# Keys and values of a linear attention laid out as head by 64 partitions with nine tokens each

## The chip, the cores and the metric

The kernel runs on one core of a Trainium2 chip. The metric is the device time of one execution in microseconds; the median of several runs counts. A core has five engines with queues of their own: PE (matrix products; PEld is its weight load), DVE (vector), ACT (scalar functions), POOL and SP. SP issues the transfers that this kernel makes between the chip's main memory and the core's, which has 128 partitions. PE writes its products to PSUM, in banks of 512 fp32 numbers a partition.

## What is computed

The attention is linear: `k` is normalized by a softmax along the 576 tokens, `q` along the 64 features, and a 64x64 matrix `kv` stands between them. The result feeds two dense stages of experts.

```python
# q, k, v: (4, 8, 576, 64): batch, heads, tokens, features
q_s = exp(q - max(q, axis=-1)); q_s = q_s / (sum(q_s, axis=-1) + 1e-09)
k_s = exp(k - max(k, axis=2));  k_s = k_s / (sum(k_s, axis=2) + 1e-09)
kv = einsum('bhsd,bhse->bhde', k_s, v)         # sum over the tokens s: (b, h, 64, 64)
attn = einsum('bhsd,bhde->bhse', q_s, kv)
x = attn.transpose(0, 2, 1, 3).reshape(2304, 512)
x = ((x @ w1) * (x @ w2)) @ w3 @ w_out         # 512 -> 1024 -> 1024 -> 512
p = probs / (sum(probs, axis=-1) + 1e-09)
out = sum over the 4 experts e of p[:, e] * (relu(x @ w1[e]) @ w2[e])
```

## The kernel before

The heads are worked on in pairs `hp`, four pairs to a batch `b`, in the order `PAIRS = [0, 2, 1, 3]`. Each pair passes through these steps.

- `load_k` and `load_v` bring keys and values. Partition p holds tokens 4p to 4p+3 of both heads, 512 numbers; the 64 tokens left over stand in a fifth place `[0:KX, :, KR]` of partitions 0 to 63, by a transfer of their own. Each value tile has a column of ones behind the 64 features (written by POOL), so that the product gives the softmax's sum along with `kv`. In batch 0 the values go to a staging tile `vs` first, and ACT copies them.
- `k_max` takes the maximum over the tokens: three maxima on DVE (L239, L243, L244) leave 128 numbers a partition, PE transposes them (L246), DVE reduces them to one column (L250), PE spreads this column over all partitions by a product with the identity (L252), and ACT copies it to `mx` (L258).
- `k_exp` subtracts `mx` (DVE, L270) and takes the exponential (ACT, L273), twice each, for the four places and the fifth.
- `k_v` (batches 0 and 1) sums `kv` of both heads in five products of 128x128 weights by 130 columns, the two diagonal blocks of which are used. `k_v2` (batches 2 and 3, `JOINED = 2`) takes two pairs together, in twenty products with 64 columns of weights (L321), one head to each half of the array's columns. Their order is fixed by `after_inst`.

DVE then adds 1e-9 to the sums and inverts them, ACT scales the blocks into `bd`, and `x_stage` multiplies `bd` by the transposed queries (L405). Where a step stands in the program is set by slots: `K_SLOT`, `Q_SLOT` and `X_SLOT` give each batch's slots, `put` enters a step there, and between the slots' steps lie the dense products. Batch 0 runs alone at the start. Batch 1 runs among the first products `ab` (x by w1 and w2), while DVE and ACT convert and split the weights `f` into `wg` (L144 to L155, L103, L104). Batches 2 and 3 run among the products `y`. `mm3` makes each of these products as three (L109 to L111), for a high and a low part of the operands. Within this a scheduler of the compiler chooses each engine's order by its own estimate of times; `hold` and `after_inst` add edges to it. SP's queue holds all loads in their order. `keep_busy` issues products on ones among the steps of batch 0.

## Time and profile before

| what | value |
|---|---|
| median of 3 runs | 1141.66 us (1141.65 to 1142.82) |
| profiled execution | 1142.81 us, its span 1141.0 us |
| granted clock of PE, mean | 0.995 |
| attention, batch 0 | to about 32 us |
| batch 1, among the products `ab` | about 32 to 98 us |
| batch 2, among `W` and `y` | about 147 to 250 us |
| batch 3, among `ab` and `y` | about 250 to 305 us |
| experts | from about 424 us |

The busy share of an engine says how near it is to setting the time of a stage; the chain of waits says which work ended last. A row of the timeline gives start and length of one run of like instructions. Products are pipelined, so lengths overlap, and what a product costs is read from the starts of the products around it. The start of a product that follows one of another kind is modelled early; the sum over a few products is sound. A product in fp32 shows as two.

### The profile page before, as it was taken

The page shows a single profiled execution, that of the slowest core. Times are in us where ns is not written, and L with a number is a line of the kernel's source. Part 1 is how long each engine was busy: PE and PEld are TensorE (multiplying, and loading weights), DVE is VectorE, ACT ScalarE, POOL GpSimd, SP SyncE. Part 2 cuts the span into 40 slices and gives each one's busy share as a digit, 9 for nine tenths or more (in the row PEclk, how much of TensorE's full clock was granted, in tenths as well). Part 3 has the DMA queues.
Part 4 walks back from the last instruction along what each step waited for, and adds up shares of the span by engine and source line. Part 5 has one row for each costly group of instructions (what it writes and reads, how often), then busy time and mean ns, then how long its engine had stood idle before and what let it go on. Part 6 is the DMA issues. An engine that isn't in the chain of part 4 may idle for free.

```text
span 1141.0 us, 18926 instructions
## 1 busy us (share of the span) xinstructions
PE 1120.9 (98%) x7159; PEld 1044.8 (92%) x7159; DVE 869.1 (76%) x1460; ACT 534.7 (47%) x974; POOL 11.4 (1%) x54
## 2 busy tenths in 40 slices
PE   7899999999999999999999999999999999999998
PEld 5677888878888889999999999999999999999998
DVE  7999696856565527999989997777779877777777
ACT  4775245745453326645555444444435434443441
POOL 0000000000010000000000000000000000000000
PEclk8999999999999999999999999999999999999999
DMA  9987962899989768777777888777777797777774
GB/s 266 269 334 289 294 174 83 222 339 396 338 283 396 301 240 311 285 281 272 290 262 289 290 305 289 248 256 251 253 253 249 251 307 249 254 251 250 253 246 128
DMA packets 124667, 308.04 MB, mean 270 GB/s; under 512 B 27936, under 2 KB 51488, under 8 KB 124576
## 3 DMA queue, kind: packets, MB, share of 16 engines
q1 hardware_dynamic: 123616, 306.04, 77.9%
q8 instruction: 57, 0.93, 0.3%
q10 hardware_dynamic: 960, 0.79, 0.3%
q14 instruction: 34, 0.28, 0.1%
HBM read 230.24 MB, written 76.55 MB: 269 GB/s over the span
## 4 chain that ended last, share of the span: by engine, by line
PE 91%; DVE 4%; DMA 3%; SPq 1%; issue 1%; ACT 0%; DVEq 0%; ACTq 0%
PE hp L976 30%; PE op L1053 29%; PE ab L111 5%; PE ab L110 5%; PE ab L109 5%; PE y L110 3%; PE y L111 3%; PE y L109 3%; PE W L109 1%; PE W L110 1%; PE W L111 1%; DMA eg<-e_b 1%; PE xp L405 1%; DMA vt<-in_v_dram 1%; PE kv L294 1%
## 5 line engine op out<-in xcount | busy, mean ns | idle before, releaser
L1053 PE MATMUL op<-eg,h 128*128 128x256 f32 x3024 | 379.8, 280 | 0.8 <-DMA eg<-e_b 0.8
L976 PE MATMUL hp<-t,eg 128*128 128x384 f32 x2016 | 376.9, 336 | 0.9 <-DVE acc L1034 0.9
L1053 PEld LDWEIGHTS op<-eg,h 128*128 128x128 f32 x3024 | 373.5, 188 | 1.2 <-PE hp L976 1.1
L976 PEld LDWEIGHTS hp<-t,eg 128*128 128x128 f32 x2016 | 344.6, 188 | 2.9 <-DVE acc L1034 1.8
L1034 DVE SCALAR_TENSOR_TENSOR acc<-op,prob,acc 128x256 f32<-128x256 f32 (+1 forms) x399 | 197.9, 525 | 42.0 <-PE op L1053 41.9
L103 ACT ACTIVATE h<-blk 128x768 fp32r<-128x768 f32 x168 | 138.0, 843 | 143.1 <-DVE blk L673 108.9
L104 DVE TENSOR_TENSOR h<-blk,h 128x768 fp32r<-128x768 f32 x168 | 157.2, 951 | 24.4 <-ACT h L103 24.3
L959 ACT ACTIVATE blk<-hp 128x384 f32<-128x384 f32 x192 | 90.4, 489 | 141.6 <-PE hp L976 138.1
L963 DVE TENSOR_TENSOR blk<-hp,blk 128x384 f32<-128x384 f32 x144 | 79.3, 556 | 67.0 <-PE hp L976 66.6
L109 PE MATMUL ab<-x,wg 128*128 128x512 f32 (+1 forms) x320 | 120.0, 378 | 1.5 <-ACT bd L308 1.1
L110 PE MATMUL ab<-x,wg 128*128 128x512 f32 (+1 forms) x320 | 118.6, 371 | 1.6 <-ACT x L426 1.4
L111 PE MATMUL ab<-x,wg 128*128 128x512 f32 (+1 forms) x320 | 117.9, 371 | 0.3 <-DVE wg L104 0.3
L965 ACT ACTIVATE blk<-blk 128x768 f32<-128x768 f32 x72 | 60.6, 845 | 73.0 <-DVE blk L963 71.3
L673 DVE TENSOR_TENSOR blk<-blk 128x768 f32<-128x768 f32 x96 | 91.4, 952 | 0.5
L110 PEld LDWEIGHTS ab<-x,wg 128*128 128x128 f32 x320 | 60.3, 189 | 13.1 <-ACT x L426 3.0
L109 PEld LDWEIGHTS ab<-x,wg 128*128 128x128 f32 x320 | 60.1, 189 | 12.7 <-ACT bd L308 1.3
L111 PEld LDWEIGHTS ab<-x,wg 128*128 128x128 f32 x320 | 60.3, 189 | 10.5 <-DVE wg L104 0.7
L567 DVE TENSOR_TENSOR ah<-ab,ah 128x512 f32<-128x512 f32 (+1 forms) x40 | 25.2, 631 | 39.3 <-PE ab L111 39.3
L104 DVE TENSOR_TENSOR eo<-e2r,eo 128x512 fp32r<-128x512 f32 x56 | 37.7, 683 | 20.0 <-ACT eo L103 19.8
L111 PE MATMUL y<-h,W 128*128 128x512 f32 x128 | 50.4, 397 | 0.0
L110 PE MATMUL y<-h,W 128*128 128x512 f32 x128 | 50.4, 394 | 0.0
L109 PE MATMUL y<-h,W 128*128 128x512 f32 x128 | 49.2, 401 | 0.0
(107 smaller groups left out, 1004.2 us busy)
## 6 DMA issues: line engine op xcount, KB each, us to landing
eg<-e_t SPq DMA_DIRECT2D x96, 512.0 KB, 4.5
eg<-e_b SPq DMA_DIRECT2D x72, 512.0 KB, 5.0
eg<-e_s SPq DMA_DIRECT2D x68, 512.0 KB, 4.4
eg<-e_a SPq DMA_DIRECT2D x51, 512.0 KB, 4.6
wg<-w SPq DMA_DIRECT2D x44, 512.0 KB, 8.3
f<-in_moe_w_dram SPq DMA_DIRECT2D x32, 512.0 KB, 6.7
e_t<-eo SPq DMA_DIRECT2D x32, 512.0 KB, 7.5
e_s<-eg SPq DMA_DIRECT2D x28, 512.0 KB, 4.5
```

The costliest lines, as they stand in the source:

```text
L103: i = nc.scalar.activation(out=hi, in_=src, func=ACTF.Copy)
L104: j = eng.tensor_tensor(out=lo, in0=src, in1=hi.bitcast(F32), op=ALU.subtract)
L109: nc.tensor.matmul(out=ps, lhsT=w_hi, rhs=r_hi, start=first, stop=False, **kw)
L110: nc.tensor.matmul(out=ps, lhsT=w_hi, rhs=r_lo, start=False, stop=False, **kw)
L111: return nc.tensor.matmul(out=ps, lhsT=w_lo, rhs=r_hi, start=False, stop=last, **kw)
L673: return lambda: nc.vector.tensor_tensor(out=dst, in0=x, in1=y, op=op)
L959: nc.scalar.activation(out=block(name)[:, u], in_=src, func=func)
L963: nc.vector.tensor_tensor(out=x[:, u], in0=src, in1=x[:, u], op=ALU.add)
L965: nc.scalar.activation(out=x, in_=x, func=ACTF.Relu)
L976: nc.tensor.matmul(out=q, lhsT=w[:, sw, kt, P * u:P * u + P], rhs=t[b][:, kt, st], start=new and kt == 0 and i == 0, stop=kt == 1 and i == ...
L1034: nc.vector.scalar_tensor_tensor(out=dst, in0=src, scalar=prob[:, T, e:e + 1], in1=dst, op0=ALU.mult, op1=ALU.add,)
L1053: nc.tensor.matmul(out=q[:, c:c + DH], lhsT=g[:, sh, u, P * i:P * i + P], rhs=w[:, sw, u], start=new and u == 0 and j == 0, stop=u == 1 an ...
```

## The change

Partition 64h + p now holds the nine tokens 9p to 9p+8 of head h of the pair, 576 numbers without a rest.

- Transfers: one for keys and one for values of a pair. A partition's keys are 2304 bytes in a row. The staging tile of batch 0 is one for each pair.
- Maximum: one reduction over the nine tokens, which reads `p r d` as `p d r`, so with steps of 64 numbers. The transposed result has 64 rows; its reduction gives a column for each head, and two products of 64x64 spread them, each on its half of the partitions.
- One subtraction and one exponential a pair.
- `kv`: 18 products of 64x64 weights by 65 columns a pair, with head h on half h of the array's rows and of its columns. One function serves one pair (batches 0 and 1) or two (2 and 3). The products stay chained, now within a pair.
- POOL no longer clears the rest's padding.

```diff
     def load_k(b, hp):
-        t = ap_.tile([P, 2, KR + 1, D], F32, tag="kr", name="kr", bufs=4)
-        src = k[b, 2 * hp:2 * hp + 2]
+        t = ap_.tile([P, QR, D], F32, tag="kr", name="kr", bufs=4)
         hold("pace" if b > 2 else ("in", b), nc.sync.dma_start(
-            out=t[:, :, 0:KR], in_=src[:, 0:KR * P].rearrange("h (p r) d -> p h r d", p=P)
-        ))
-        hold("pace" if b > 2 else ("in", b), nc.sync.dma_start(
-            out=t[0:KX, :, KR], in_=src[:, KR * P:S].rearrange("h p d -> p h d")
+            out=t, in_=k[b, 2 * hp:2 * hp + 2].rearrange("h (p r) d -> (h p) r d", p=QP)
         ))
         kraw[b, hp] = t
 
-    staged = {}
-
     def load_v(b, hp):
-        t = ap_.tile([P, 2, KR + 1, D + 1], F32, tag="vt", name="vt", bufs=4)
+        t = ap_.tile([P, QR, D + 1], F32, tag="vt", name="vt", bufs=4)
         nc.gpsimd.memset(t[..., D:D + 1], 1.0)
-        if b >= JOINED:
-            nc.gpsimd.memset(t[KX:P, :, KR, 0:D], 0.0)
-        src = v[b, 2 * hp:2 * hp + 2]
+        src = v[b, 2 * hp:2 * hp + 2].rearrange("h (p r) d -> (h p) r d", p=QP)
+        x = t[..., 0:D]
         if b in V_WHOLE:
-            i = PAIRS.index(hp)
-            if i % 2 == 0:
-                staged[b] = raw("vs")
-            x = staged[b][:, 512 * (i % 2):512 * (i % 2) + 512].rearrange(
-                "p (h r d) -> p h r d", h=2, d=D
-            )
-            hold(("in", b), nc.sync.dma_start(
-                out=x, in_=src[:, 0:KR * P].rearrange("h (p r) d -> p h r d", p=P)
-            ))
-            nc.scalar.activation(out=t[:, :, 0:KR, 0:D], in_=x, func=ACTF.Copy)
-        for h in range(0 if b in V_WHOLE else 2):
-            hold("pace" if b > 2 else ("in", b), nc.sync.dma_start(
-                out=t[:, h, 0:KR, 0:D], in_=src[h, 0:KR * P].rearrange("(p r) d -> p r d", p=P)
-            ))
-        hold("pace" if b > 2 else ("in", b), nc.sync.dma_start(
-            out=t[0:KX, :, KR, 0:D], in_=src[:, KR * P:S].rearrange("h p d -> p h d")
-        ))
+            x = raw("vs")[:, 0:QR * D].rearrange("p (r d) -> p r d", d=D)
+        hold("pace" if b > 2 else ("in", b), nc.sync.dma_start(out=x, in_=src))
+        if b in V_WHOLE:
+            nc.scalar.activation(out=t[..., 0:D], in_=x, func=ACTF.Copy)
         vt[b, hp] = t
...
     def k_max(b, hp):
-        kr = kraw[b, hp]
-        m4 = ap_.tile([P, 2, 2, D], F32, tag="m2", name="m2", bufs=1)
-        i = hold(("k", b, PAIRS.index(hp)), nc.vector.tensor_tensor(
-            out=m4, in0=kr[:, :, 0:2], in1=kr[:, :, 2:4], op=ALU.max
+        m2 = ap_.tile([P, D], F32, tag="mf", name="mf", bufs=2)
+        hold(("k", b, PAIRS.index(hp)), nc.vector.tensor_reduce(
+            out=m2, in_=kraw[b, hp].rearrange("p r d -> p d r"), axis=AX.X, op=ALU.max
         ))
-        m2 = ap_.tile([P, 2, D], F32, tag="mf", name="mf", bufs=2)
-        nc.vector.tensor_tensor(out=m2, in0=m4[:, :, 0], in1=m4[:, :, 1], op=ALU.max)
-        nc.vector.tensor_tensor(out=m2[0:KX], in0=m2[0:KX], in1=kr[0:KX, :, KR], op=ALU.max)
         ps = bank(ps_a, "mt")
-        i = nc.tensor.transpose(ps[:, 0:P], m2.rearrange("p h d -> p (h d)"), ident)
+        i = nc.tensor.transpose(ps[0:D, 0:P], m2, ident)
         if b == 0:
             keep_busy(FILL_T[PAIRS.index(hp)], i)
-        mt = ap_.tile([P, 1], F32, tag="mt", name="mt", bufs=2)
-        nc.vector.tensor_reduce(out=mt, in_=ps[:, 0:P], axis=AX.X, op=ALU.max)
-
-        i = nc.tensor.matmul(
-            out=ps[:, P:2 * P], lhsT=mt.to_broadcast([P, P]), rhs=ident, start=True, stop=True
-        )
+        mt = ap_.tile([D, 2, 1], F32, tag="mt", name="mt", bufs=2)
+        nc.vector.tensor_reduce(
+            out=mt, in_=ps[0:D, 0:P].rearrange("d (h p) -> d h p", h=2), axis=AX.X, op=ALU.max
+        )
+        for h in range(2):
+            i = nc.tensor.matmul(
+                out=ps[D * h:D * h + D, P:P + D], lhsT=mt[:, h].to_broadcast([D, D]),
+                rhs=ident[0:D, 0:D], start=True, stop=True,
+            )
         if b == 0:
             keep_busy(FILL_B[PAIRS.index(hp)], i)
-        mx = ap_.tile([P, 2, 1, D], F32, tag="mx", name="mx", bufs=2)
-        nc.scalar.activation(
-            out=mx.rearrange("p h r d -> p (h r d)"), in_=ps[:, P:2 * P], func=ACTF.Copy
-        )
+        mx = ap_.tile([P, 1, D], F32, tag="mx", name="mx", bufs=2)
+        nc.scalar.activation(out=mx[:, 0], in_=ps[:, P:P + D], func=ACTF.Copy)
         mxk[b, hp] = mx
 
     def k_exp(b, hp):
         kr, mx = kraw.pop((b, hp)), mxk.pop((b, hp))
-        t = ap_.tile([P, KR + 1, 2, D], F32, tag="ek", name="ek", bufs=2)
-        if b >= JOINED:
-            nc.gpsimd.memset(t[KX:P, KR], 0.0)
-        for p, r0, n in ((P, 0, KR), (KX, KR, 1)):
-            x = kr[0:p, :, r0:r0 + n]
-            hold(("e", b, PAIRS.index(hp)), nc.vector.tensor_tensor(
-                out=x, in0=x, in1=mx[0:p].to_broadcast([p, 2, n, D]), op=ALU.subtract
-            ))
-            nc.scalar.activation(
-                out=t[0:p, r0:r0 + n].rearrange("p r h d -> p h r d"), in_=x, func=ACTF.Exp
-            )
+        t = ap_.tile([P, QR, D], F32, tag="ek", name="ek", bufs=2)
+        hold(("e", b, PAIRS.index(hp)), nc.vector.tensor_tensor(
+            out=kr, in0=kr, in1=mx.to_broadcast([P, QR, D]), op=ALU.subtract
+        ))
+        nc.scalar.activation(out=t, in_=kr, func=ACTF.Exp)
         ekt[b, hp] = t
...
-    def k_v(b, hp):
-        ek, vv = ekt.pop((b, hp)), vt.pop((b, hp))
-        bd = empty_bd()
-        ps = bank(ps_w if b == 0 else ps_a, "kv")
-        for r in range(KR + 1):
-            p = P if r < KR else KX
-            i = nc.tensor.matmul(
-                out=ps[:, 0:2 * D + 2], lhsT=ek[0:p, r].rearrange("p h d -> p (h d)"),
-                rhs=vv[0:p, :, r, :], start=r == 0, stop=r == KR,
-            )
-        if b == 0:
-            keep_busy(FILL_V[PAIRS.index(hp)], i)
-        rs = ap_.tile([P, 1], F32, tag="rs", name="rs", bufs=2)
-        nc.vector.tensor_scalar(
-            out=rs, in0=ps[:, D:D + 1], scalar1=1e-9, scalar2=None, op0=ALU.add
-        )
-        nc.vector.reciprocal(out=rs, in_=rs)
-        for h in range(2):
-            p = slice(D * h, D * h + D)
-            o = (D + 1) * h
-            nc.scalar.activation(
-                out=bd[p, D * h:D * h + D], in_=ps[p, o:o + D], func=ACTF.Copy, scale=rs[p]
-            )
-        kvb[b, hp] = bd
-
-    def k_v2(b, j):
-        ps = bank(ps_a, "kv").rearrange("p (w c) -> p w c", c=P)
-        bds, last = [], None
-        for hh in range(2):
-            bds.append(empty_bd())
-            ek, vv = ekt.pop((b, 2 * hh + j)), vt.pop((b, 2 * hh + j))
-            for r in range(KR + 1):
+    def k_v(b, *pairs):
+        ps = bank(ps_w if b == 0 else ps_a, "kv").rearrange("p (w c) -> p w c", c=P)
+        n = len(pairs)
+        for w, hp in enumerate(pairs):
+            ek, vv, last = ekt.pop((b, hp)), vt.pop((b, hp)), None
+            for r in range(QR):
                 for h in range(2):
+                    p = slice(D * h, D * h + D)
                     i = nc.tensor.matmul(
-                        out=ps[D * h:D * h + D, hh, 0:D + 1], lhsT=ek[:, r, h], rhs=vv[:, h, r],
-                        start=r == 0, stop=r == KR, skip_group_check=hh > 0,
+                        out=ps[p, w, 0:D + 1], lhsT=ek[p, r], rhs=vv[p, r],
+                        start=r == 0, stop=r == QR - 1, skip_group_check=w > 0,
                     )
                     if last is not None:
                         after_inst(i, last)
                     last = i
-        rs = ap_.tile([P, 2, 1], F32, tag="rs2", name="rs", bufs=2)
+        if b == 0:
+            keep_busy(FILL_V[PAIRS.index(hp)], i)
+        rs = ap_.tile([P, n, 1], F32, tag=f"rs{n}", name="rs", bufs=2)
         nc.vector.tensor_scalar(
-            out=rs, in0=ps[:, 0:2, D:D + 1], scalar1=1e-9, scalar2=None, op0=ALU.add
+            out=rs, in0=ps[:, 0:n, D:D + 1], scalar1=1e-9, scalar2=None, op0=ALU.add
         )
         nc.vector.reciprocal(out=rs, in_=rs)
-        for hh in range(2):
+        for w, hp in enumerate(pairs):
+            kvb[b, hp] = empty_bd()
             for h in range(2):
                 p = slice(D * h, D * h + D)
                 nc.scalar.activation(
-                    out=bds[hh][p, p], in_=ps[p, hh, 0:D], func=ACTF.Copy, scale=rs[p, hh]
+                    out=kvb[b, hp][p, p], in_=ps[p, w, 0:D], func=ACTF.Copy, scale=rs[p, w]
                 )
-            kvb[b, 2 * hh + j] = bds[hh]
...
             elif i % 2:
-                put(mid, s + 1, k_v2, b, i // 2)
+                put(mid, s + 1, k_v, b, PAIRS[i - 1], hp)
```

In the order of SP at the start of the program, these are the transfers of keys (`kr`), queries (`qr`), values (`vs`, `vt`) and of the first weights (`f`). Before:

```order
L186 DMA kr<-in_k_dram 128x2x256
L189 DMA kr<-in_k_dram 64x2x64
L186 DMA kr<-in_k_dram 128x2x256
L189 DMA kr<-in_k_dram 64x2x64
L186 DMA kr<-in_k_dram 128x2x256
L189 DMA kr<-in_k_dram 64x2x64
L186 DMA kr<-in_k_dram 128x2x256
L189 DMA kr<-in_k_dram 64x2x64
L230 DMA qr<-in_q_dram 64x2x576 x4
L209 DMA vs<-in_v_dram 128x2x256
L217 DMA vt<-in_v_dram 64x2x64
L495 DMA f_134<-in_moe_w_dram 128x4x256 x2
```

After:

```order
L184 DMA kr<-in_k_dram 128x576 x4
L209 DMA qr<-in_q_dram 64x2x576 x4
L196 DMA vs<-in_v_dram 128x576
L442 DMA f_129<-in_moe_w_dram 128x4x256 x2
L196 DMA vs<-in_v_dram 128x576 x3
```

Four transfers ahead of the queries are gone, and one between the queries and the first weights.

On PE, in batch 3 where the maxima `mt` of one pair are transposed and spread among the products `ab`. Before:

```order
L111 MATMUL ab<-x_1_969,wg 128x512
L405 MATMUL xp<-qT,bd 128x288
L246 MATMUL mt<-ident,mf 128x128
L109 MATMUL ab<-x_3_1029,wg 128x512 x2
L252 MATMUL mt<-ident,mt 128x128
L110 MATMUL ab<-x_3_1029,wg 128x512
L111 MATMUL ab<-x_3_1029,wg 128x512
```

After (L108 to L110 are now the dense products, L221 the transpose, L229 the spreading):

```order
L110 MATMUL ab<-x_1_1023,wg 128x512
L352 MATMUL xp<-qT,bd 128x288
L221 MATMUL mt<-ident,mf 64x128
L108 MATMUL ab<-x_3_1083,wg 128x512 x2
L229 MATMUL mt<-ident,mt 64x64 x2
L221 MATMUL mt<-ident,mf 64x128
L109 MATMUL ab<-x_3_1083,wg 128x512
```

The steps stand between dense products as before; the spreading is two products, both steps are of tiles of another size, and the next pair's transpose has come forward.

On PE, where the first two pairs of batch 2 are summed, between the products that make `W` and the first `y`. Before:

```order
L111 MATMUL W<-wg 128x512
L321 MATMUL kv<-vt,ek 64x65 x9
L541 MATMUL W<-W,nident 128x512
L321 MATMUL kv<-vt,ek 64x65
L541 MATMUL W<-W,nident 128x512
L246 MATMUL mt<-ident,mf 128x128
L541 MATMUL W<-W,nident 128x512 x2
L109 MATMUL y_1818<-h,W 128x512
```

After (L266 is `kv`, L488 what was L541):

```order
L110 MATMUL W<-wg 128x512
L266 MATMUL kv<-vt,ek 64x65 x9
L488 MATMUL W<-W,nident 128x512
L266 MATMUL kv<-vt,ek 64x65
L488 MATMUL W<-W,nident 128x512
L266 MATMUL kv<-vt,ek 64x65 x3
L488 MATMUL W<-W,nident 128x512
L266 MATMUL kv<-vt,ek 64x65 x7
L488 MATMUL W<-W,nident 128x512
L266 MATMUL kv<-vt,ek 64x65 x7
L221 MATMUL mt<-ident,mf 64x128
L108 MATMUL y_1854<-h,W 128x512
```

Before, ten of the twenty products stand here in two pieces, and ten ran further up. Now 27 of 36 stand here, in five pieces with a dense product between each two.

## Rows read from the trace of the kernel before

**Rows 1.** The page: busy time of each engine, PE by slices, the chain by engine.
```profile
PE 1120.9 (98%) x7159; PEld 1044.8 (92%) x7159; DVE 869.1 (76%) x1460; ACT 534.7 (47%) x974; POOL 11.4 (1%) x54
...
PE   7899999999999999999999999999999999999998
...
PE 91%; DVE 4%; DMA 3%; SPq 1%; issue 1%; ACT 0%; DVEq 0%; ACTq 0%
```
**Rows 2.** Stages: length, busy PE, PEld, DVE, ACT, POOL, clock, DMA, GB/s.
```profile
3.60:33.10 29.50, 23.31 (x106) 17.07 (x105) 24.55 (x51) 16.54 (x39) 0.46 (x4) 0.83 1.05 286
33.10:64.60 31.50, 27.85 (x133) 21.01 (x134) 29.74 (x53) 21.16 (x52) 0.32 (x2) 1.00 1.05 301
64.60:98.20 33.60, 31.47 (x151) 24.99 (x149) 29.60 (x55) 24.80 (x80) 1.71 (x8) 1.00 0.71 266
200.00:240.00 40.00, 40.00 (x218) 32.92 (x218) 32.24 (x60) 24.45 (x54) 1.48 (x10) 1.00 0.87 256
```
**Rows 3.** Start: SP's issues (timeline), the chain, DVE's first row on queries, a stage.
```profile
0.75 0.46 SPq L186 DMA_DIRECT2D kr<-in_k_dram  x1
...
5.94 2.56 SPq L230 DMA_DIRECT2D qr<-in_q_dram  x4
...
6.59 5.11 DMA qr<-in_q_dram
...
11.79 1.35 DVE L345 TENSOR_REDUCE qm<-qr 128x18 f32<-128x1152 f32 x1 [1.54 <-DMA qr<-in_q_dram]
...
2.00:8.00 6.00, 5.13 (x25) 3.44 (x23) 3.31 (x11) 0.61 (x3) 0.07 (x1) 1.00 0.80 206
```
**Rows 4.** Timeline of DVE in batch 1: start, length, line, operation, output from input.
```profile
41.29 0.41 DVE L239 TENSOR_TENSOR m<-kr 128x256 f32<-128x256 f32 x1
41.63 1.21 DVE L151 SCALAR_TENSOR_TENSOR f<-f,f 128x1024 int32<-128x1024 int32 x1
42.76 0.28 DVE L243 TENSOR_TENSOR mf<-m 128x128 f32<-128x128 f32 x1
42.97 0.28 DVE L250 TENSOR_REDUCE mt<-mt 128x1 f32<-128x128 f32 x1
...
46.92 0.88 DVE L270 TENSOR_TENSOR kr<-kr,mx 128x512 f32<-128x512 f32 x2
47.72 0.68 DVE L104 TENSOR_TENSOR wg<-f,wg 128x512 fp32r<-128x512 f32 x1
```
**Rows 5.** Timeline of PE round a joined block of batch 2, and its first part.
```profile
232.61 0.39 PE L110 MATMUL y<-h,W 128*128 128x512 f32 x1
232.93 1.39 PE L321 MATMUL kv<-vt,ek 128*64 128x65 f32 x40
...
234.59 0.40 PE L109 MATMUL y<-h,W 128*128 128x512 f32 x1
...
232.93 0.57 PE L321 MATMUL kv<-vt,ek 128*64 128x65 f32 x12
```
**Rows 6.** Timeline of PE in batch 1: a pair's products and the next row.
```profile
74.44 1.47 PE L294 MATMUL kv<-vt,ek 128*128 128x130 f32 x10
75.84 0.55 PE L392 MATMUL qt<-ident,qe 128*128 128x128 f32 x3
```
**Rows 7.** Timeline of PE in batch 2: transposes, and a broadcast.
```profile
216.12 0.39 PE L111 MATMUL y<-h,W 128*128 128x512 f32 x1
216.35 0.49 PE L392 MATMUL qt<-ident,qe 128*128 128x128 f32 x3
...
216.91 0.27 PE L246 MATMUL mt<-ident,mf 128*128 128x128 f32 x1
...
217.25 0.39 PE L111 MATMUL y<-h,W 128*128 128x512 f32 x1
...
224.37 0.39 PE L110 MATMUL y<-h,W 128*128 128x512 f32 x1
224.59 0.38 PE L252 MATMUL mt<-ident,mt 128*128 128x128 f32 x2
...
225.05 0.39 PE L110 MATMUL y<-h,W 128*128 128x512 f32 x1
```

More of the change, by code (lines that the diff above doesn't have):

```diff
@@ L70, in linear_attention_moe_kernel @@
     NC = len(chunks)
-    KR, KX = 4, S - 4 * P
     NE1, NOUT = 1, 5
```

## The prediction, made before the changed kernel ran

> **What bounds the kernel now.** I read the page first, for the share of each engine and for the chain of waits. PE is busy 1120.9 us of 1141.0, nine tenths or more in every slice from the third to the last but one, and 91% of the chain that ended last is PE's [rows 1]. So after the start, each ns added to PE's queue is a ns of the end, and a ns taken from DVE, ACT, POOL or SP is worth nothing. Then I read the table by stages. It says from when this holds. In 200 to 240 us, where batch 2 of the attention runs between the products `y`, PE is busy 40.00 of 40.00. In 33.1 to 64.6 us it is not: PE 27.85 of 31.50, DVE 29.74. There DVE sets the pace, since it splits the weights `wg` that the products `ab` wait for. In 64.6 to 98.2 the two are close, PE 31.47 and DVE 29.60 of 33.60 [rows 2]. Batch 0 and batch 1 of the attention lie in this front part, batches 2 and 3 in the part that PE fills. Each term below is therefore counted twice over: as DVE and DMA time in front, as PE time behind.
>
> **Term 1, the transfers at the start.** SP issues eight transfers of keys before the first of the queries: the first begins at 0.75, the queries' at 5.94, so (5.94 - 0.75) / 8 = 0.65 us each. The queries land at 11.70, and DVE waits 1.54 us for them before 11.79 [rows 3]. After the change there are four issues fewer, and the queries go out 4 x 0.65 = 2.6 us earlier. They need not land that much earlier, because the engines of the DMA were then 0.80 busy in 2 to 8 us [rows 3]: only 6.0 x 0.20 = 1.2 us were free. The gain lies between 1.2 and 2.6 us; I take **-2.0**, nearer the issue's end, because the joined transfers also have longer pieces (2304 bytes a partition instead of 1024 and 256). Behind that the front has DVE idle of 29.50 - 24.55 = 4.95 us in 3.6 to 33.1 and 1.76 us in 33.1 to 64.6 [rows 2]. If the earlier transfers removed all of that, the gain of terms 1 and 2 would be 6.7 + 1.6 = 8.3; this is the bound from below. The staged values of batch 0 now take a granule each, four instead of two. SP's order at the start still has the weights' transfers at the same distance, so I count that at nothing; if it cost something, DVE's splitting would wait for `f`.
>
> **Term 2, DVE in front.** Three maxima become one reduction of 576 elements. By starts of successive rows the 128x256 maximum takes 41.63 - 41.29 = 0.34, and each 128x128 one 42.97 - 42.76 = 0.21, so the three take about 0.75 [rows 4]. What one reduction costs an element comes from two lengths, 0.28 us for 128 [rows 4] and 1.35 for 1152 [rows 3]: (1.35 - 0.28) / 1024 = 1.045 ns. The new one then takes 0.21 + 448 x 1.045 ns = 0.68. The subtractions take 47.72 - 46.92 = 0.80 as two [rows 4]; one of 576 is again 0.68. That is -0.07 and -0.12, about -0.2 a pair, and with eight pairs in front **-1.6**, all of it on the path where DVE paces. The price rests on one choice. The new reduction reads every 64th element (256 bytes apart), and no row of before reads like that. The nearest is the row of 41.63, whose operand takes every second element: 1.21 us for 1024, 1.18 ns an element and thus the plain rate [rows 4]. The bounds are the plain rate and twice the time per element, 576 x 1.045 ns = +0.60 us a pair, +4.8 over the eight. I take the plain rate, since the only stepped row shows it.
>
> A rule speaks against that choice: the Trainium skill, "Advanced Engine Details and Errata", section "SBUF Cachelines", says that lines have 16 bytes, that two hits a line are needed for full speed, and that another line at each access costs a penalty, without a figure. The row of 41.63 agrees in that its operand meets each line twice; it doesn't show the case here. By the rule the second of the two ends would hold, and it is a rival below.
>
> **Term 3, PE in front.** The products of a pair in batch 1 took 75.84 - 74.44 = 1.40 to 1.47 us for ten passes (a product in fp32 shows as two) [rows 6]. They become 36 passes of 64x64 by 65. For their price I take batch 2's block, 40 passes in column tiles. Its rows show the whole as 1.39 us and the first twelve passes as 0.57, so a pass costs (1.39 - 0.57) / 28 = 0.0293 us, tiles of the two heads running side by side. The block costs more than its passes: from the `y` product at 232.61 to that at 234.59, with one other `y` product in between that is left out, 1.98 us go by, and two `y` products take 2 x 0.227, so the block costs 1.53. 40 x 0.0293 = 1.17 is the passes, and **0.36 is the way into the tiles and out** [rows 5]. After: 36 x 0.0293 + 0.36 = 1.41, no change against 1.40 to 1.47. New are the small blocks: transposes with weights of 64 columns and broadcasts of 64x64, some eight of them in batch 1, 8 x 0.36 = +2.9, less some 0.1 for each of four broadcasts. Of this +2.4 the pauses of PE in front (3.65 us in 33.1 to 64.6, 2.13 in 64.6 to 98.2 [rows 2]) take more than half: **+1.0**, between 0 and 2.4. Batch 0's products fall in 3.6 to 33.1, where PE has pauses too: nothing.
>
> **Term 4, PE behind.** Eight pairs in batches 2 and 3, no pause to hide anything. Passes: 18 products of two, times eight, 288, against 160 before: 128 x 0.0293 = **+3.75**. Broadcasts: from 224.37 to 225.05 two `y` products and one broadcast take 0.68, so it cost 0.68 - 0.454 = 0.226; the new one, four passes of 64, about 0.12: 8 x -0.11 = **-0.87** [rows 7]. The transposes: from 216.12 to 217.25 go three `y` products and four transposes (three `qt`, one `mt`), (1.13 - 0.68) / 4 = 0.113 each, so before the change a transpose pays nothing to get in or out [rows 7]; the new ones have as many columns to move. But transpose and broadcast now have another tile size than the `y` products on both sides. By the order of PE's queue, stretches of tiles number 8 before (of `kv` alone) and 22 after: 14 x 0.36 = **+5.0**, and some 0.4 for changes between 128x64 and 64x64 within a stretch. The ends: a change of size may cost nothing for a lone product (its own part 3.75 - 0.87 + 2 x 0.36 = +3.6), or the whole (+8.3). I take the whole, **+8.3**, by the row of the block that shows it.
>
> **The sum:** -2.0 - 1.6 + 1.0 + 8.3 = +5.7. On the profiled run of 1142.81 us that is 1148.5. This run stood 1.1 above the median of 1141.66; on the median it is 1147.4, and I forecast **1147.5**. Nothing later takes it back, since PE has no free slice behind [rows 1].
>
> **The rivals.** All times stand on the median.
> *The stepped maximum runs at half speed.* For it: no row shows such a step. Against: the step of two costs nothing. +4.8 in front: 5.7 + 4.8 = +10.5, 1152.2. Chance 0.23.
> *The tiles of the two heads do not run side by side.* The new ones stand on different rows and columns of the array and share one bank; before, only tiles on different columns are seen to overlap. A pass would cost 0.0586, so +288 x 0.0293 = 8.4 behind, and some 1.8 in front: +15.9, 1157.6. Chance 0.09. The Trainium skill, "TensorEngine Tiling (Array Packing)", section "Gotcha 1: PSUM Pressure", says that different row tiles cannot use the same bank at once; no row of before has row tiles.
> *Not slower: changing the tile size costs nothing for lone products.* Then batch 1 gives -0.6, batches 2 and 3 +3.6, and the front's -3.6 decides: -0.6, 1141. With the front at its bound it is -8.3 - 0.6 + 3.6 = -5.3, 1136.4. It decides from the point where the 22 new stretches, 8 in front and 14 behind, cost under 0.36 - 5.7 / 22 = 0.10 us each. For it: the transposes before cost 0.113 between products of another shape. Against: their tile size was the same. Chance 0.24, 0.17 of it faster, the rest within the bound of no change.
> *The front gains up to its idle time, and PE pays as forecast:* -8.3 + 9.3 = +1.0, 1142.7. Against: DVE was busy 0.94 of 33.1 to 64.6, with little idle left to gain. Chance 0.08.
>
> **How the numbers follow.** The forecast has 0.36, with 1144 to 1151 around it. A change within 0.2% is within 2.3 us, about what a measurement of this kernel can tell from none. Faster: 0.17 + 0.03 = 0.20, from the third rival and the fourth. Same: 0.02 + 0.07 + 0.05 = 0.14, from the lower edge of the forecast, the third rival and the fourth. Slower: 0.34 + 0.23 + 0.09 = 0.66. The range goes from 1138.5, in the midst of the third rival, to 1154.5, above the half-speed maximum; left out are the overlap rival (0.09) and half of the faster cases (0.10), 2 in 10 together.
>
> **What would show it.** Term 1: the first reduction of the queries begins near 9.8. Term 2: the new maximum lasts 0.75 us; 1.3 or more is the first rival. Term 4: in 200 to 300 us a joined block of 72 passes costs 72 x 0.0293 + 0.36 = 2.47 between `y` products, 4.6 without overlap; a lone transpose costs near 0.47 instead of 0.113, and 0.113 again is the third rival. I am wrong altogether if batch 1's stage ends by 5 us or more earlier, or if the time from 305 us to the end changes.

## The result and the profile after

The changed kernel takes 1150.68 us in the median (1149.19 to 1156.46, six runs) against 1141.66 before. The ratio is 1.0085, 95% interval 1.0063 to 1.0107, so it is slower by 7 to 12 us. The forecast was 1147.5 with a range of 1138.5 to 1154.5. The profiled execution took 1149.58 us, 6.8 more than the profiled one of before, which in turn stood 1.1 above its own median.

The page of the changed kernel, in the same lines as [rows 1]:

```profile
PE 1124.6 (98%) x7527; PEld 1046.0 (91%) x7527; DVE 875.1 (76%) x1412; ACT 533.0 (46%) x958; POOL 7.8 (1%) x38
...
PE   6989999999999999999999999999999999999998
...
PE 91%; DVE 3%; DMA 3%; issue 1%; ACT 1%; SPq 0%; DVEq 0%; ACTq 0%
```

PE still sets the end. Its 368 further instructions are passes of `kv` (576 instead of 240) and of the spreading (64 instead of 32). The stages, in the columns of [rows 2]:

```profile
3.60:33.10 29.50, 21.62 (x215) 16.21 (x213) 27.41 (x41) 16.38 (x32) 0.45 (x4) 0.65 1.10 312
33.10:64.60 31.50, 29.68 (x178) 22.21 (x177) 30.07 (x44) 21.68 (x62) 0.12 (x1) 1.00 1.01 310
64.60:98.20 33.60, 29.35 (x223) 23.16 (x222) 27.63 (x48) 22.44 (x70) 0.34 (x3) 1.00 0.65 238
200.00:240.00 40.00, 40.00 (x277) 31.67 (x273) 32.62 (x52) 23.78 (x48) 0.56 (x5) 1.00 0.84 232
```

From 64.6 to 98.2 us PE has 4.25 us of pauses, 2.13 before, and the clock granted in the first stage is 0.65, 0.83 before. To see where the time went I took the starts of the 1352 fp32 products of 512 columns, which both kernels run in the same number, from the two traces:

| product | before, us | after, us | later by |
|---|---|---|---|
| 1st | 32.29 | 34.86 | 2.57 |
| 81st | 65.09 | 63.41 | -1.68 |
| 101st | 69.77 | 72.13 | 2.36 |
| 201st | 105.16 | 105.08 | -0.08 |
| 401st | 150.77 | 150.68 | -0.09 |
| 801st | 255.07 | 260.11 | 5.04 |
| 1101st | 336.80 | 343.06 | 6.26 |
| 1352nd | 424.07 | 430.37 | 6.30 |

Between the profiled executions the whole difference arises from 150 to 310 us, in batches 2 and 3. In front the sign changes three times and nothing is left at 105 us. Between the 81st and the 101st product 4 us are lost at once; 2.2 of them are one pause of PE, shown below, and the rest is work of the attention that stood elsewhere in PE's order before. All pauses of PE in 36 to 106 us together come to 4.9 us, and to 5.0 before, so in this execution the pauses have moved and not grown.

### The profile page after: what moved, and what is told of

The parts are those of the page before. It is cut to its first block, busy times and chain, and to the rows that moved or that the text cites. A ratio compares the mean times of both kernels' runs of the same rounds, so it can differ in the third digit from the quotient of the medians.

```text
span 1147.4 us, 19524 instructions
## 1 busy us (share of the span) xinstructions
PE 1124.6 (98%) x7527; PEld 1046.0 (91%) x7527; DVE 875.1 (76%) x1412; ACT 533.0 (46%) x958; POOL 7.8 (1%) x38
## 4 chain that ended last, share of the span: by engine, by line
PE 91%; DVE 3%; DMA 3%; issue 1%; ACT 1%; SPq 0%; DVEq 0%; ACTq 0%
PE hp L923 30%; PE op L1000 28%; PE ab L109 6%; PE ab L110 6%; PE ab L108 6%; PE y L108 3%; PE y L110 3%; PE y L109 3%; PE W L108 1%; PE xp L352 1%; PE W L109 1%; PE W L110 1%; PE kv L266 1%; DMA qr<-in_q_dram 1%; DVE acc L981 1%; DMA f<-in_moe_w_dram 1%
## 5 line engine op out<-in xcount | busy, mean ns | idle before, releaser
L108 PE MATMUL ab<-x,wg 128*128 128x512 f32 (+1 forms) x320 | 119.7, 377 | 0.4 <-ACT x L102 0.2
L110 PE MATMUL ab<-x,wg 128*128 128x512 f32 (+1 forms) x320 | 117.5, 371 | 0.0
L108 PEld LDWEIGHTS ab<-x,wg 128*128 128x128 f32 x320 | 60.0, 189 | 10.6 <-ACT x L102 0.6
L110 PEld LDWEIGHTS ab<-x,wg 128*128 128x128 f32 x320 | 60.4, 189 | 9.9
L110 PE MATMUL y<-h,W 128*128 128x512 f32 x128 | 49.7, 394 | 0.0
L108 PE MATMUL y<-h,W 128*128 128x512 f32 x128 | 48.4, 401 | 0.0
```

The lines of the kernel that those rows point to most:

```text
L108: nc.tensor.matmul(out=ps, lhsT=w_hi, rhs=r_hi, start=first, stop=False, **kw)
L110: return nc.tensor.matmul(out=ps, lhsT=w_lo, rhs=r_hi, start=False, stop=last, **kw)
```

## Experiments

Theory A: behind, PE pays 6 to 7 us for `kv` and the spreading; in front the gains of the prediction don't come, and what the medians show beyond that (9.0 - 6.3 = 2.7 us) is a pause of PE at 67 us. Its rivals were the speed of the stepped maximum, and interaction of front and back.

**The changed kernel again.** No edit.

> The changed kernel once more, beside the others on one chip. If the 9.0 us between the medians are the changed kernel's own and not one chip's, the ratio is 1.006 to 1.010 again; if the profiled execution (6.8 us slower) is the rule and the rest scatter, it is nearer 1.006. The dense products of 310 us and later should stand about 6 us later than in the kernel before, those of 100 to 150 us not later.

1151.37 us, ratio 1.0085 (1.0072 to 1.0098): the slowdown is the kernel's own. The profiled execution was this time a longer one, 1154.16 us, and its 201st dense product came 2.11 us later than before. PE's stages (columns as in [rows 2]) say where:

```profile
66.00:70.00 4.00, 2.02 (x12) 1.32 (x10) 3.20 (x5) 3.99 (x24) 0.00 (x0) 1.00 0.65 251
70.00:72.00 2.00, 1.76 (x37) 1.67 (x38) 1.97 (x3) 1.95 (x5) 0.11 (x1) 0.83 0.89 299
72.00:74.00 2.00, 2.00 (x8) 1.51 (x7) 2.00 (x6) 1.87 (x5) 0.00 (x0) 0.50 1.01 377
74.00:76.00 2.00, 2.00 (x10) 1.65 (x9) 1.93 (x5) 1.59 (x5) 0.00 (x0) 0.82 0.87 348
```

After a pause in 66 to 70 us the granted clock, the third number from the end, falls to 0.50, the lower of the two levels, and comes back at 75 us. In the first profile of the same kernel the same pause was there and the clock stayed at 1.00:

```profile
72.00:74.00 2.00, 2.00 (x12) 1.70 (x11) 2.00 (x6) 1.87 (x5) 0.00 (x0) 1.00 0.99 393
```

So the expectation for the products of 100 to 150 us, not later, did not hold in this execution. Its span is 4.6 us above the first profile's. Up to the 201st product it loses 2.2 of them, 0.5 before the pause and some 1.6 behind it with the half clock; up to the 1352nd another 1.2; and 1.2 in the experts. The half clock at 72 us is thus a third of what sets this execution apart. Of the 1.2 in the middle 0.76 are one wait of PE for split weights:

```profile
175.23 0.74 PE L110 MATMUL W<-wg 128*128 128x512 f32 x2 [0.76 <-DVE wg L103]
```

**The new layout in front alone, and behind alone.**

```diff
+    def load_k(b, hp):
+        (o_load_k if b >= 2 else n_load_k)(b, hp)
...
-                put(mid, s + 2, k_v, b, hp)
+                put(mid, s + 2, o_k_v if b >= 2 else n_k_v, b, hp)
```

The other functions of a pair are chosen likewise, `o_` from before, `n_` from after; for behind alone the condition is `b < 2`.

> The new layout in batches 0 and 1 alone, batches 2 and 3 as before. Theory A (all that shows is PE's work behind, the front comes out even because the earlier queries and the slower maximum cancel): within 2 us of the kernel before. Theory B (the front costs what the medians show beyond the profiled shift behind, 9.0 - 6.3): 2 to 3 us slower, 1144 to 1145. If the prediction's terms 1 to 3 were right: 2.6 us faster.

> The new layout in batches 2 and 3 alone, batches 0 and 1 as before. Theory A and B: the whole of the shift seen between 140 and 310 us, +6.3, so 1148, with no shift before 140 us. If front and back interact (other buffers free, another order), less or more than what is left of the changed kernel's 9.0 beside the run with the new front.

Front alone: 1144.20 us, ratio 1.0023 (1.0015 to 1.0032), 2.5 us slower. Behind alone: 1148.77, ratio 1.0062 (1.0050 to 1.0074), 7.0 us slower. Their sum, 9.5, is what the whole change costs (9.0 and 9.6), so no interaction of the two parts shows. Theory B of the expectations holds for the front: it is a loss, where the prediction had a gain of 2.6. The eleven executions with the new front go with their clock, from 1142.83 us at a mean of 0.994 to 1146.54 at 0.989. The profiled one is the fastest of them, and its 201st product comes at 105.01, no later than before: where the slower ones lose their time no trace shows. In the whole changed kernel mean clock and time don't go together as well (1149.58 us at 0.990, 1151.58 at 0.992).

**Maxima on contiguous rows, and a maximum with a step of one.**

```diff
-        hold(("k", b, PAIRS.index(hp)), nc.vector.tensor_reduce(
-            out=m2, in_=kraw[b, hp].rearrange("p r d -> p d r"), axis=AX.X, op=ALU.max
-        ))
+        hold(("k", b, PAIRS.index(hp)), nc.vector.tensor_tensor(
+            out=m4, in0=kr[:, 0:4], in1=kr[:, 4:8], op=ALU.max
+        ))
+        nc.vector.tensor_tensor(out=m4[:, 0:2], in0=m4[:, 0:2], in1=m4[:, 2:4], op=ALU.max)
+        nc.vector.tensor_tensor(out=m2, in0=m4[:, 0], in1=m4[:, 1], op=ALU.max)
+        nc.vector.tensor_tensor(out=m2, in0=m2, in1=kr[:, 8], op=ALU.max)
```

```diff
-            out=m2, in_=kraw[b, hp].rearrange("p r d -> p d r"), axis=AX.X, op=ALU.max
+            out=m2, in_=kraw[b, hp].rearrange("p r d -> p (r d)").rearrange("p (d r) -> p d r", r=QR), axis=AX.X, op=ALU.max
```

> The changed kernel with the stepped reduction replaced by four maxima on contiguous rows (256, 128, 64 and 64 elements). By the rows of before they take about 0.34 + 0.21 + 0.13 + 0.13 = 0.8 us where the stepped one takes 1.05 from start to start, so 0.25 us a pair. Theory A: DVE sets the front's pace, eight pairs give 2 us. Rival: the front is paced by the transfers of the weights or by PE, and the time stays within 0.5 us. Either way the stall of 0.6 us at 259 us, where the spreading waits behind the next pair's maximum, should shrink.

> The changed kernel with the maximum taken over nine neighbouring numbers instead of over every 64th; it leaves out the maximum over the tokens as such and takes another one of the same count and shape. If the step makes the reduction slow, it now lasts 0.75 us instead of 1.12. If its 64 short groups of nine do (the reduction of the queries has 18 groups of 64), it stays at 1.12.

The line of the maximum on DVE, with shortest, median and longest duration in ns, in the changed kernel and with the step of one:

```profile
L217 DVE TENSOR_REDUCE mf<-kr x16: 1118/1144/1225, 3.7 to 259.5; 128x64 f32<-128x576 f32 x16
```

```profile
L217 DVE TENSOR_REDUCE mf<-kr x16: 729/742/753, 3.6 to 260.3; 128x64 f32<-128x576 f32 x16
```

The step costs 0.40 us of 1.14, and the groups of nine cost nothing: 0.74 is what the prediction had for the plain rate. The time does not follow. With the step of one a single execution took 1150.89 us, and the contiguous maxima gave 1153.51 (ratio 1.0097, 1.0079 to 1.0115), where the changed kernel took 1151.37 beside them; their six executions go from 1149.68 to 1156.69. Neither forecast has come, the 2 us of theory A or the 0.5 of its rival. The slowest has a mean clock of 0.998, so it is not the half clock; the cause stays open, as only the fastest has a trace.

The traces show no gain either. From the 1st to the 81st dense product 28.59 us go by with the step of one and 28.45 with the contiguous maxima, 28.55 in the changed kernel, all at a granted clock of 1.00. Theory A's claim that DVE's speed in the maxima sets the front's end has fallen. Of the rival the cause stands, for in 45 to 65 us of the changed kernel PE is busy 19.83 of 20.00 us and DVE 19.07. The 1st product itself comes 0.76 and 1.58 us earlier than in the changed kernel, but the clock granted in 3.6 to 33.1 us was 0.83 and 1.00 in these two executions and 0.65 in that one, so this can't be put down to DVE. PE's two waits of 0.3 us at the maxima at 259 us are gone with the contiguous ones, as expected.

With the contiguous maxima PE again has a pause behind the 18 exponentials, now for the copy to `mx`, as the table of its waits in 64 to 72 us shows (us, times, longest):

```profile
PE mt L226 <- ACT mx L241: 1.8, 1, 1.8
```

**Where the pause comes from: another bank.**

```diff
-        ps = bank(ps_w if b == 0 else ps_a, "kv").rearrange("p (w c) -> p w c", c=P)
+        ps = bank(ps_w if b < 2 else ps_a, "kv").rearrange("p (w c) -> p w c", c=P)
```

In the changed kernel the timelines of PE and of ACT at the pause read:

```profile
67.15 0.33 PE L229 MATMUL mt<-ident,mt 64*64 64x64 f32 x4
69.66 1.26 PE L266 MATMUL kv<-vt,ek 64*64 64x65 f32 x36 [2.17 <-issue]
...
68.61 0.34 ACT L300 ACTIVATE qe<-qr,qm 128x64 f32<-128x64 f32 x1
68.85 0.19 ACT L300 ACTIVATION_READ_ACCUMULATOR qe<-qr,qm 128x1 f32 x1
68.94 0.62 ACT L284 ACTIVATE bd<-kv,rs 64x64 f32<-64x64 f32 x2
69.58 0.63 ACT L102 ACTIVATE wg<-f 128x512 fp32r<-128x512 f32 x1
```

The products of one pair start 0.10 us after ACT has emptied the bank of another (68.94 + 0.62 = 69.56). That copy stood on ACT behind the 18 exponentials that do the second block of batch 1's queries. The profile names no releaser for PE, so I gave `kv` other banks.

> The changed kernel with batch 1's kv in the other pool of banks, so that a pair's products need not wait until ACT has emptied the bank of an earlier pair behind its 18 exponentials for the queries (the pause of PE of 2.2 us at 67 us). Theory A: this pause, and the half clock that follows it in some executions (2.1 us in one of two profiles), is the 2.5 us that the new front costs; then the pause is gone and the median falls by 2 to 3 us, to 1148.5. Rival: the pause only takes the place of waits for the split weights, and the front's end does not move: 1151. The order on PE changes with it by the scheduler's choice.

> The new layout in batches 0 and 1 alone, as in the run with the new front, and batch 1's kv in the other pool of banks. Theory A (the new front's 2.5 us are the wait for a bank behind ACT's 18 exponentials, and the half clock that follows in some executions): 1.5 to 2.5 us less than with the new front alone, so 1141.7 to 1142.7, and executions within 0.6 us of each other as with the bank changed in the whole kernel. Rival (the gain of the other bank in the whole kernel came from the other order behind): 1144 and a spread of 3 us again.

> The kernel before with batch 1's kv in the other pool of banks, as a control. Its kv in batch 1 waits 0.5 us at most, so theory A says within 1 us of the kernel before, 1141 to 1142.5. If it gains 1.5 us or more as well, the bank is a matter of either kernel and says nothing on the new front.

In the whole changed kernel: 1149.40 us, all five executions within 1149.12 to 1149.54, ratio 1.0065 (1.0052 to 1.0077); the 201st dense product came 0.98 us earlier than before. With the new front alone: 1141.73, ratio 0.9996 (0.9987 to 1.0005), 2.5 us less than without the other bank. So the front's loss goes with this edit. Its executions lie within 3.1 us, though, and not within 0.6 as theory A wanted, so the small spread of the whole kernel is not shown to be the bank's.

Nor is the waiting gone. With the other bank the pair's products no longer wait, but what stands behind them in PE's queue does (the changed kernel with the other bank, 64 to 76 us):

```profile
PE ab L108 <- ACT wg L102: 1.0, 1, 1.0
PE qt L339 <- DVE qe L327: 0.5, 1, 0.5
```

Both come from ACT's 18 exponentials again: the split stands behind them on ACT, and DVE scales their results. The 101st dense product is no earlier (72.77 us against 72.13, with three more transposes before it). Over 36 to 106 us PE's pauses come to 3.2 us in both runs with the other bank, against 4.9 in both without. That is 1.7 us less, of the 2.5 in the median; that the rest is the half clock, which the profiles with the other bank don't have here, is argued and not shown.

The control warns as well. The kernel before with the other bank is slower, 1144.76 us (1.0023, 1.0014 to 1.0033), which theory A had not expected. Its timelines show why:

```profile
68.75 1.14 PE L294 MATMUL kv<-vt,ek 128*128 128x130 f32 x7
72.05 0.63 PE L109 MATMUL ab<-x,wg 128*128 128x512 f32 x1 [2.17 <-ACT bd L308]
...
71.39 0.62 ACT L308 ACTIVATE bd<-kv,rs 64x64 f32<-64x64 f32 x2
72.03 0.63 ACT L273 ACTIVATE ek<-kr 128x512 f32<-128x512 f32 x1
```

The other pool is one from which dense products `ab` take their banks too. Here a dense product has come to stand behind the same copy, and a pause of 2.17 us is there, this time with its releaser named; the dense product after it lasts 0.63 instead of 0.39, and the clock of 65 to 98 us is 0.95. The bank is therefore not the matter in itself. It is whether something of PE's comes to wait for what stands on ACT behind the exponentials.

**Without the 18 exponentials.**

```diff
-ON_SCALAR = {(1, 1)}
+ON_SCALAR = set()
```

> The changed kernel with that alone, its bank as it was. Theory A: the pause of 2.2 us at 67 us, in which PE waits for a bank that ACT empties behind the 18 exponentials, goes, and with it the half clock that followed: 1148.5 to 1149.5 and executions within 0.6 us of each other, as with the other bank. Rival: the 2.7 us on DVE replace it: 1151 to 1153.

> The new layout in batches 0 and 1 alone with batch 1's kv in the other pool of banks, and the second block of batch 1's queries done as all others (a subtraction and a sum on DVE, 1.35 and 1.33 us, one exponential on ACT) instead of 18 exponentials on ACT. Theory A: the pauses of PE at 67 to 73 us behind ACT's exponentials go, and what DVE gets in addition fits its slack after 65 us (3 to 4 us): 1 to 2 us less than 1141.73, so 1140 to 1141, faster than the kernel before. Rival: DVE sets the pace there and its 2.7 us come out at the end: 1143 to 1144.5.

In the changed kernel: 1149.94 us, ratio 1.0078 (1.0063 to 1.0094). The trace has no wait of PE's queue in 64 to 72 us, and the 201st dense product comes 0.83 us earlier than before. So the pause hangs on the exponentials, and DVE's additional 2.7 us did not come out at the 201st product. A gain in time is not shown: the interval covers the changed kernel's 1.0085, the median lies between the two forecasts, and the executions still differ, from 1148.74 to 1153.67. With the new front alone and the other bank: 1142.05, ratio 1.0004 (0.9993 to 1.0015), again between the forecasts. No version beat the kernel before by more than the measurement can tell.

**The tiles: spreading with full columns, and one head after the other.**

```diff
-                out=ps[D * h:D * h + D, P:P + D], lhsT=mt[:, h].to_broadcast([D, D]),
+                out=ps[:, P + D * h:P + D * h + D], lhsT=mt[:, h].to_broadcast([D, P]),
...
-        nc.scalar.activation(out=mx[:, 0], in_=ps[:, P:P + D], func=ACTF.Copy)
+        for h in range(2):
+            p, o = slice(D * h, D * h + D), P + D * h
+            nc.scalar.activation(out=mx[p, 0], in_=ps[p, o:o + D], func=ACTF.Copy)
```

```diff
-            for r in range(QR):
-                for h in range(2):
+            for h in range(2):
+                for r in range(QR):
```

> The changed kernel with the maxima spread by two products of 64x128 weights (all 128 columns of the array, both heads' maxima on all partitions) instead of two of 64x64, and two copies on ACT instead of one. Theory A: what a stretch of tiles pays beyond its passes, 0.35 us, comes from tiles on part of the columns that return to full width; then a lone spreading costs 4 x 0.03 = 0.12 to 0.23 us instead of 0.46, eight give about 2 us behind, and the time is near 1149.5. Rival: any tile smaller than the array pays; then it stays at 0.46 and the time at 1151. The transposes, whose tile is 128x64, cost 0.113 as before in the changed kernel, which speaks against the plain rival.

> The changed kernel with the 18 products of a pair in another order: the nine of one head, then the nine of the other, instead of in turn. If products of the two heads run side by side only since they follow each other on different rows and columns, a pass costs 0.058 us instead of 0.029: a joined block of 72 takes 4.5 us between the dense products instead of 2.45, and the part behind grows by 8 us. If the overlap does not hang on the order (or 0.029 is what one pass takes alone), the block stays at 2.45.

PE's timeline round a joined block of batch 3 and round a lone spreading, first in the changed kernel:

```profile
306.54 0.39 PE L110 MATMUL y<-h,W 128*128 128x512 f32 x1
306.85 2.32 PE L266 MATMUL kv<-vt,ek 64*64 64x65 f32 x72
...
309.44 0.40 PE L109 MATMUL y<-h,W 128*128 128x512 f32 x1
...
211.84 0.39 PE L110 MATMUL y<-h,W 128*128 128x512 f32 x1
212.16 0.33 PE L229 MATMUL mt<-ident,mt 64*64 64x64 f32 x4
...
212.76 0.40 PE L109 MATMUL y<-h,W 128*128 128x512 f32 x1
```

Then the block with one head after the other, and the spreading with full columns:

```profile
314.87 0.39 PE L110 MATMUL y<-h,W 128*128 128x512 f32 x1
315.18 3.88 PE L266 MATMUL kv<-vt,ek 64*64 64x65 f32 x72
...
319.33 0.39 PE L109 MATMUL y<-h,W 128*128 128x512 f32 x1
```

```profile
211.47 0.61 PE L110 MATMUL y<-h,W 128*128 128x512 f32 x2
212.01 0.66 PE L229 MATMUL mt<-ident,mt 64*128 64x64 f32 x4
...
212.93 0.40 PE L109 MATMUL y<-h,W 128*128 128x512 f32 x1
```

In each case one `y` product between is left out, so 0.454 us are the dense ones'. The block costs 2.90 - 0.45 = 2.45 in turn and 4.46 - 0.45 = 4.01 in sequence. The heads' products do overlap, and it is the order in turn that lets them: in the trace the passes of the two heads start 0.006 us apart and such a pair every 0.058 us, while within one head a single pass starts every 0.058 us. That 4.01 came and not 4.5 is since some passes still overlap where the head changes. The kernel with the heads in sequence took 1160.18 us in its one execution.

The spreading costs 0.92 - 0.45 = 0.47 with 64x64; with weights of 64x128 it is 212.93 - 211.47 = 1.46 for three `y` products of 0.227 and the spreading, so 0.78. The time rose to 1157.17 (1.0133, 1.0118 to 1.0149). Theory A on tiles is refuted in its cause, but the sum has two parts. With 64x128 weights the passes start every 0.11 us, so 0.44 of the 0.78 are passes, and 0.34 remain; with 64x64 two pairs take 0.12 of the 0.47, and 0.35 remain. Weights over all columns make each pass dearer and the edges of the stretch no cheaper. What exactly is paid for at the edges stays open. (The eight spreadings behind are 8 x 0.31 = 2.5 us of the some 5.5 by which the ratios differ. The edit also adds a copy on ACT for each pair, and its 1st dense product comes 2.4 us later than the changed kernel's.)

## Why the prediction was right, and where not

The direction was right, and for the reason given: behind, PE has no pause, and `kv` and the spreading cost it more. That the time lay within the range is in part luck. The forecast of +5.8 was short of +9.0, and its parts were off on both sides: by the runs with one part alone the front cost 2.5 us where 2.6 were to be gained, and the part behind 7.0 where 8.3 were to be paid. The two errors partly cancel.

*Term 4, behind, +8.3: right in its mechanism, too large by a part.* In the first profile it is +6.35 (6.26 at the 1101st product, -0.09 at the 401st). I read each insertion between dense products off the trace, as above. `kv` costs 12.1 us instead of 7.8: +4.3, for a forecast of 3.75 and two more stretches. The joined block measured 2.45 for a forecast of 2.47, and 1.52 before [rows 5]; one pass is again (2.45 - 1.52) / 32 = 0.029. Lone spreadings cost 0.46 to 0.47, as 4 passes and 0.36 had it, and 0.226 before [rows 7]: +1.65 for the eight, since one of them stands within a block. The rest, some 0.4, is waits. The term that was mis-sized is the transposes. I had them pay for another tile size, and they don't:

```profile
146.56 0.39 PE L110 MATMUL W<-wg 128*128 128x512 f32 x1
146.79 0.38 PE L221 MATMUL mt<-ident,mf 128*64 128x128 f32 x2
146.93 0.47 PE L108 MATMUL ab<-x,wg 128*128 128x512 f32 x1
147.24 0.39 PE L109 MATMUL ab<-x,wg 128*128 128x512 f32 x1
```

Two transposes with 128x64 weights and two dense products take 0.68, so 0.11 us a transpose as in [rows 7]. The rival "changing the tile size costs nothing" was right on half of its stretches. In other executions the shift behind is larger: 7.6 us from the 201st to the 1352nd product with the new layout behind alone, and as much in the second profile of the changed kernel, where 0.76 of the excess is the wait at 175 us shown above.

*Term 1, the transfers, -2.0: the sign came, its worth did not show.* The rows of the changed kernel that answer to [rows 3]:

```profile
2.61 2.70 SPq L209 DMA_DIRECT2D qr<-in_q_dram  x4
...
9.79 1.33 DVE L292 TENSOR_REDUCE qm<-qr 128x18 f32<-128x1152 f32 x1
```

The queries' reduction begins at 9.79 instead of 11.79, 2.0 us earlier as I had it. The exact number is luck: its row shows no wait for a transfer, DVE was busy with its own maxima up to there, and the queries' transfers begin 3.3 us earlier (2.61 against 5.94) and not 2.6. And the first dense product comes 2.57 us later. I had put batch 0's PE work at nothing, and PE does run it at the half clock for longer (0.65 against 0.83 in 3.6 to 33.1). The clock alone is not the cause: with 0.77 in that stretch the first dense product came at 34.75 us with the new layout in front and at 32.72 with the old one. PE also waits longer for ACT's copies to `x` just ahead of it, first after and then before:

```profile
34.65 0.37 PE L369 MATMUL xp<-x,nident 128*128 128x224 f32 x1 [1.16 <-ACT x L368]
```

```profile
31.84 0.62 PE L422 MATMUL xp<-x,nident 128*128 128x288 f32 x2 [0.42 <-ACT x L421]
```

*Term 2, DVE, -1.6: mis-sized, with the wrong sign.* The stepped maximum takes 1.14 us, between my two bounds (0.75 and 1.35). The section "SBUF Cachelines" of "Advanced Engine Details and Errata" in the Trainium skill had warned of a penalty, and the runs agree, with 0.40 us on 0.74. From start to start it takes 1.05 where the three maxima of before took 0.75, and the subtraction 0.66 where the two took 0.80: +0.16 a pair, so +1.3 for the eight by this working, and not -1.6.

```profile
12.97 0.75 DVE L242 TENSOR_TENSOR kr<-kr,mx 128x576 f32<-128x576 f32 x1
13.63 1.35 DVE L307 TENSOR_TENSOR qr<-qr,qm 128x1152 f32<-128x1152 f32 x1
...
28.83 1.13 DVE L217 TENSOR_REDUCE mf<-kr 128x64 f32<-128x576 f32 x1
29.88 1.21 DVE L154 SCALAR_TENSOR_TENSOR f<-f,f 128x1024 int32<-128x1024 int32 x1
```

The other step of the argument that failed is "all of it on the path": to take the 0.40 us off each maximum again gained nothing from the 1st to the 81st dense product and did not make the kernel faster.

*Term 3 and the front's sum, -2.6: failed.* The front alone is +2.5. What I left out is the order. I had counted PE's pauses as room for the new work, and did not ask what of PE's work would wait behind ACT's 18 exponentials. A pause of 2.2 us stands there now. In the profiles whose clock stays up it only takes the place of other pauses (4.9 us in all, 5.0 before); in others the half clock follows it. Giving `kv` another bank took 1.7 us of pauses and 2.5 us of time away. What part of the front's loss is the half clock's, no run separates.

*The rivals.* The time, 1150.68, is nearer to the 1152.2 of the stepped maximum at half speed than to the forecast, but not for that rival's reason: the maximum is slowed by half and not doubled, and no run with a faster one was faster beyond the noise. The overlap rival is out: 2.45 against 4.01. The Trainium skill's rule in "TensorEngine Tiling (Array Packing)", "Gotcha 1: PSUM Pressure", that different row tiles can't use one bank at once, does not describe what this kernel shows: two tiles on different rows and columns wrote to different partitions of one bank, and their passes started 0.006 us apart. The measurement decides.

## What to carry to other kernels

Where PE is always busy, count its passes and its stretches of small tiles, and take the price of a stretch from a row of the very shape: here the spreading paid at its edges and the transpose did not. The rest of a tidier layout is worth nothing there. Where it is not, a shorter instruction on another engine is no gain until one has looked at what each engine's queue puts ahead of the copies and splits that PE waits for. Splitting a change by stage (new in front, new behind) is a quick way to see which term of a sum has failed.

## What the runs showed of the hardware

- A lone stretch of four passes costs 0.47 us with 64x64 tiles (the changed kernel) and 0.78 with 64x128 weights (the run with full columns), some 0.35 of it beyond the passes in both; a transpose with 128x64 weights costs 0.11, as one of full width before.
- Products of 64x64 on two diagonal tiles run side by side when they alternate: 72 passes take 2.45 us in turn (the changed kernel) and 4.01 in sequence (head by head).
- A maximum over every 64th fp32 number takes 1.14 us (the changed kernel) where one over neighbouring numbers takes 0.74 (the step of one).
- After the same pause of 2.2 us the granted clock fell to 0.50 in the second profile of the changed kernel and to 0.52 with the step of one, and stayed at 1.00 in the first profile.
